# A weight load on SyncE that waits for the landing of the load two places ahead

## Chip, core and metric

The kernel runs on one core of one Trainium2 chip. The metric is the device time of one execution in microseconds; the time before is the median of three runs.

## What is computed

Attention with pooled queries, then a mixture of experts over its output. Queries are averaged in pairs, so 1152 positions give 576 tokens in each of 2 batches, 1152 tokens of width 512. Each token goes to the one expert with the largest gate logit; an expert takes at most 288 tokens.

```python
q_pool = q.reshape(B, H, S // factor, factor, D).mean(axis=3)
scores = scale * np.matmul(q_pool, k.transpose(0, 1, 3, 2))
attn = softmax(scores)
x = np.matmul(attn, v)                      # -> (N=1152, D=512)
expert_idx = np.argmax(x @ w_gate, axis=1)
gate_w = softmax(x @ w_gate)[range(N), expert_idx]
# the first `capacity` (288) tokens of each of the E=8 experts
h = np.maximum(np.einsum('ecd,edf->ecf', disp, w1), 0.0)   # w1: 8 x 512 x 1024
y = np.einsum('ecf,efd->ecd', h, w2)                       # w2: 8 x 1024 x 512
out[i] = gate_w[i] * y[expert_idx[i], pos[i]]
```

## The kernel before

The program has two parts. The first, to about 342 us, is the attention: TensorE makes scores by thirds of a row, ScalarE exponentiates, TensorE turns the result and multiplies it with v. At its end each token's expert and slot are computed, and GpSimd scatters the tokens into `xs`, a table in DRAM with 288 rows for each expert.

The second part goes through the eight experts in order. `load_x(e)` brings an expert's rows into `xe` (SyncE for expert 0, GpSimd for the others, three experts ahead). `unit(e, u)` computes a group of its tokens: `units` are 64, 64, 128 and 32 tokens. A unit of 64 is 32 matmuls with `w1` (line 824), 32 with `w2` (line 859), with turns of the intermediate result (line 838) and of the next expert's tokens (line 736) between them, and at its end `send`, in which GpSimd scatters the rows to `out` (line 762). Unit 0 is always computed. `later` puts every further unit under a condition (line 879): a flag that says whether the expert has that many tokens, which TensorE, ScalarE, VectorE and GpSimd each load into a register (`flags_of`, line 886). The path on which the unit is computed is the straight one; an engine that skips the rest of an expert's units takes the branch.

The weights are 32 loads of 1 MB (`chunks`), four for each expert: two halves of `w1`, two of `w2`. `load_w(i)` issues load i on SyncE into the buffer `wraw[i % NR]`, with `NR` = 16 buffers, so an expert's four buffers are used again four experts later. Loads 0 to 5 (`NR0` = 6) are issued during the attention, 6 and 7 behind them, and 8 to 15 when the token rows of expert 0 have been issued. After expert e come the loads of expert e + 4, each of which waits until the units that read its buffer are done:

```python
for e in range(E):
    ...
    later(e, 1, flags[e])
    if e + NX < E:
        load_x(e + NX)
    for i in range(4 * e + NR, min(4 * e + NR + 4, 4 * E)):
        load_w(i)
```

In the second part the order on SyncE, GpSimd, ScalarE and TensorE is that of the code (`manual_schedule`). SyncE takes no conditional branch: it only issues loads. Its DMAs go to one hardware queue (q1 in the profile); GpSimd's go to q0, and the engines' instructions come in pages of 16 and 8 KB on q8 and q14.

Of the kernel before, what the change touches and what calls it, by code (L numbers as in the profile page):

```python
# [10 lines left out]
I32 = mybir.dt.int32  # L11
# [11 lines left out]
MS = {mybir.EngineType.Pool, mybir.EngineType.SP, mybir.EngineType.Activation, mybir.EngineType.PE}  # L23
NR, NR0 = 16, 6
NX = 3
ENG = [mybir.EngineType.PE, mybir.EngineType.Activation, mybir.EngineType.DVE, mybir.EngineType.Pool]
FAR = 1.0e6
UT = 2
# [7 lines left out]
def attention_moe(ctx: ExitStack, tc, cap, q, k, v, wg, w1, w2, out):  # L36
    nc = tc.nc
# [536 lines left out]
    wraw = [wraw_p.tile([P, 4, 512], F32, name=f"wraw{i}") for i in range(NR0)]  # L574
# [7 lines left out]
    def load_w(i):  # L582
        e, m, c = chunks[i]
        if m == 0:
            src = w1[e].rearrange("(a p) f -> p a f", p=P)[:, :, c * 512:(c + 1) * 512]
        else:
            src = w2[e, c * 512:(c + 1) * 512, :].rearrange("(a p) d -> p a d", p=P)
        nc.sync.dma_start(out=wraw[i % NR], in_=src)

    def posts_run(f):  # L590
# [3 lines left out]
    with ExitStack():  # L594
# [34 lines left out]
        for n in range(-LEAD, 3 * NG + 20):  # L629
            p, i = divmod(n, NS)  # L630
# [29 lines left out]
            if 0 <= p < NP:  # L660
                for j in V0.get(i, ()) if p < NP - 1 else ():
                    todo.append(lambda j=j: pv_kt(p, 0, j))
                if i == XO0 and p < NP - 1:
                    todo.append(lambda: x_out(p, 0))
                if i == 26 and p % HP == HP - 1 and p < NP - 1:
                    todo.append(lambda b=p // HP: lambda: route(b, 0, 2))
                if p + 1 < NP:
                    pk, pq, p0 = (PK, PQ, 1) if p else (PK0, PQ0, PP0)
                    if i in pk:
                        todo.append(lambda: prep_k(p + 1, pk.index(i)))  # L670
                    if i in pq:
                        todo.append(lambda: prep_q(p + 1, pq.index(i)))
                    if i == p0:
                        prep_pool(p + 1)
                    if i == 22:
                        todo.append(lambda: prep_mix(p + 1))
                if p == 0 and i == 6:
                    todo.append(lambda: prep_mix(0))
                if i == 10 and p + 2 < NP:
                    load_pair(p + 2)  # L680
                if p in (1, 2) and i % 3 == 0:
                    fill()
                while fills and p == 2 and i == NS - 1:
                    fill()
                if p == NP - 2 and i % 2 == 0 and i // 2 < NR0:
                    load_w(i // 2)
# [28 lines left out]
    wraw += [ws_p.tile([P, 4, 512], F32, name=f"wraw{i}") for i in range(NR0, NR)]  # L715
    xes = [xe_p.tile([P, XB, ROW], F32, name=f"xe{i}") for i in range(NX)]
    xfs = [xe_p.tile([P, DC, XB * P], F32, name=f"xf{i}") for i in range(2)]
# [7 lines left out]
    def load_x(e):  # L725
        q = nc.gpsimd if e else nc.sync
        for s, c in blocks:
            r = e * cap + s
            q.dma_start(out=xes[e % NX][0:c, s // P, :], in_=xs[r:r + c, :])

    def trans_x(e, b):
        xe, xf = xes[e % NX], xfs[e % 2]
        c = blocks[b][1]
        ps = tr_ps.tile([P, 512], F32, tag="tr", name="xps")
        for d in range(DC):
            nc.tensor.transpose(ps[:, d * c:(d + 1) * c], xe[0:c, b, d * P:(d + 1) * P], ident[0:c, 0:c])
        nc.scalar.copy(xf[:, :, b * P:b * P + c], ps[:, 0:DC * c].rearrange("p (d c) -> p d c", c=c))

    def tags(e, u):
        o, n = units[u]  # L740
        xe, gt, it = xes[e % NX], gts[e % 4], ids[e % 4]
        src, b = slice(o % P, o % P + n), o // P
# [129 lines left out]
    def hint(e, u, flags):  # L872
        if u < NU:
            return lambda: tc.mark_branch_hint_location(f"u{e}_{u}", hint=flags[u - 1], engines=ENG)
        return lambda: None

    def later(e, u, flags):

        with tc.If(flags[u - 1] > 0, preferred_fallthrough_block=True, label=f"u{e}_{u}"):  # L879
            nxt = units[u + 1][0] if u + 1 < NU else 0  # L880
            unit(e, u, [lambda: trans_x(e, nxt // P)] if nxt and nxt % P == 0 else (), hint(e, u + 1, flags))
            if u + 1 < NU:
                later(e, u + 1, flags)

    def flags_of(e):
        flags.append(nc.values_load_multi_w_load_instructions(
            more_i[0:1, e, :], engines=ENG, min_val=0, max_val=1, skip_runtime_bounds_check_because="each is the outcome of a comparison"
        )[1])

    with tc.manual_schedule(engines=MS):  # L890
        flags = []
        flags_of(0)
        for i in range(NR0, NR0 + 2):
            load_w(i)
        for e in range(min(NX, E)):
            load_x(e)
        for i in range(NR0 + 2, min(NR, 4 * E)):
            load_w(i)
        trans_x(0, 0)
        for e in range(E):  # L900
            nxt = [lambda: trans_x(e + 1, 0), lambda: flags_of(e + 1)] if e + 1 < E else ()
            unit(e, 0, nxt, hint(e, 1, flags[e]))
# [5 lines that stand above are left out]
# [25 lines left out]
```

## Time and profile before

| | us |
|---|---|
| median of 3 runs (529.9, 533.02, 533.17) | 533.02 |
| the profiled execution | 532.41 |
| its span, first to last instruction | 530.7 |
| TensorE busy in the span | 480.1 (90%) |
| VectorE, ScalarE, GpSimd busy | 270.2, 249.5, 167.0 |
| mean granted TensorE clock | 0.975 |

The span is what the trace covers; 1.7 us of the profiled execution's own time lie around it. The shares are means over both parts; a change in the second part is to be read from the stages of that part. A matmul's idle time before it is what TensorE lost there, and the name behind it is what ended the wait, with "PEq" for TensorE's own sequencer and "issue" for time in which it waited for nothing that the profile shows. "Us to landing" of a DMA runs from its issue to the completion.

### The profile page before, as it was taken

Reading aid. Unit: us, or ns where it says so; the run is one execution under the profiler, and the core shown is the slowest. Engines: PE = TensorE matmul, PEld = TensorE weight load, DVE = VectorE, ACT = ScalarE, POOL = GpSimd, SP = SyncE. Lnnn points to the kernel's source line nnn. Section 1 sums busy time; section 2 is a strip of 40 time slices with the busy share of each in tenths; the row PEclk is TensorE's granted clock in tenths of the full one; section 3 lists DMA queues with packets and bytes.
Section 4 is the critical chain, followed back from the end, with each engine's and each line's share of the span. In section 5 each row is a group of like instructions: output and inputs, shape, how many; then the busy total and the mean of one; then the engine's idle time right before and its main releaser. Section 6 shows DMA issues by size and latency. Waiting matters only on the chain. (4 is left out here: it accounts for less than half of the span.)

```text
span 530.7 us, 9093 instructions
## 1 busy us (share of the span) xinstructions
PE 480.1 (90%) x3183; PEld 315.6 (59%) x3183; DVE 270.2 (51%) x725; ACT 249.5 (47%) x731; POOL 167.0 (31%) x290
## 2 busy tenths in 40 slices
PE   3798999999998997998999999897889998999993
PEld 2565766566666765765666766544545745574571
DVE  6587887687687898778678655600001010000100
ACT  5675866676675764766666767111112111211210
POOL 4385453243244255236035000323131132111200
PEclk9789999999999998999999999999799999999997
DMA  8899982033033132330210202389999257000000
GB/s 233 161 255 352 385 249 66 2 94 88 4 89 80 56 92 64 81 90 1 51 42 5 51 1 83 150 275 378 384 389 379 106 180 264 11 21 21 15 10 19
DMA packets 55737, 69.96 MB, mean 132 GB/s; under 512 B 21873, under 2 KB 32117, under 8 KB 55680
## 3 DMA queue, kind: packets, MB, share of 16 engines
q1 hardware_dynamic: 50320, 53.56, 32.9%
q0 software_dynamic: 4816, 15.66, 8.2%
q8 instruction: 32, 0.52, 0.4%
q14 instruction: 25, 0.20, 0.1%
q10 hardware_dynamic: 544, 0.02, 0.1%
HBM read 52.48 MB, written 11.98 MB: 121 GB/s over the span
## 5 line engine op out<-in xcount | busy, mean ns | idle before, releaser
L355 DVE TENSOR_REDUCE negm<-s 128x1 f32<-128x384 f32 x216 | 115.7, 553 | 66.3 <-PE s L350 63.3
L371 ACT ACTIVATE p<-s,negm 128x384 f32<-128x384 f32 x216 | 124.4, 583 | 39.5 <-DVE negm L359 34.0
L350 PE MATMUL s<-k,q 128*128 128x384 f32 x432 | 128.5, 389 | 10.0 <-ACT p L371 9.9
L388 PE MATMUL tp<-ident,p 128*128 128x128 f32 x648 | 109.1, 281 | 7.6 <-DVE pt L397 7.6
L413 PE MATMUL pv<-pt,vraw 128*64 128x256 f32 (+2 forms) x612 | 107.4, 407 | 0.0
L350 PEld LDWEIGHTS s<-k,q 128*128 128x128 f32 x432 | 68.1, 196 | 49.1 <-ACT p L371 32.9
L388 PEld LDWEIGHTS tp<-ident,p 128*128 128x128 f32 x648 | 81.0, 143 | 24.4 <-DVE pt L397 11.2
L399 ACT COPY pt<-tp 128x384 f32<-128x384 f32 (+1 forms) x160 | 69.9, 453 | 52.4 <-PE tp L388 51.0
L210 POOL TENSOR_TENSOR k<-kts,k 64x384 fp32r<-64x384 f32 x42 | 42.2, 1005 | 66.2 <-DVE k L209 40.3
L413 PEld LDWEIGHTS pv<-pt,vraw 128*64 128x64 f32 x612 | 41.9, 136 | 34.0 <-issue 19.4
L824 PE MATMUL hps<-wraw,xf 128*64 128x256 f32 (+1 forms) x448 | 53.2, 398 | 9.1 <-PEq L879 3.6
L253 POOL TENSOR_TENSOR q<-qts,q 64x256 fp32r<-64x256 f32 (+1 forms) x76 | 50.8, 675 | 18.0 <-DVE q L247 9.5
L762 POOL DMA_INDIRECT out_dram<-yo,id x17 | 17.1, 1007 | 120.9 <-issue 52.2
L859 PE MATMUL yps<-wraw,ht 128*64 128x256 f32 (+1 forms) x448 | 50.6, 385 | 1.2 <-DVE ht L841 1.2
L829 DVE TENSOR_SCALAR hs<-hps 128x256 f32<-128x256 f32 x12 | 5.1, 425 | 86.6 <-PE hps L824 86.6
L824 PEld LDWEIGHTS hps<-wraw,xf 128*64 128x64 f32 (+1 forms) x448 | 29.5, 137 | 28.6 <-issue 11.7
L371 ACT ACTIVATION_READ_ACCUMULATOR p<-s,negm 128x1 f32 x216 | 43.7, 202 | 0.0
L397 DVE COPY pt<-tp 128x384 f32<-128x384 f32 (+1 forms) x80 | 40.2, 511 | 6.2 <-PE tp L388 5.4
L247 DVE CAST q<-qts 64x256 fp32r<-64x256 f32 (+1 forms) x70 | 42.2, 617 | 1.1
L756 ACT ACTIVATE yo<-yps,gt 128x256 f32<-128x256 f32 (+1 forms) x15 | 7.8, 517 | 65.6 <-PE yps L859 37.1
L859 PEld LDWEIGHTS yps<-wraw,ht 128*64 128x64 f32 (+1 forms) x448 | 27.4, 133 | 17.0 <-issue 3.9
L431 POOL COPY sums<-sums 64x3 f32<-64x3 f32 x8 | 1.5, 183 | 76.4 <-ACT p L371 76.4
(117 smaller groups left out, 397.2 us busy)
## 6 DMA issues: line engine op xcount, KB each, us to landing
wraw<-in_moe_w_dram SPq DMA_DIRECT2D x32, 1024.0 KB, 14.6
vraw<-in_v_dram SPq DMA_DIRECT2D x8, 576.0 KB, 4.2
kc<-k SPq DMA_DIRECT2D x16, 288.0 KB, 3.7
xs<-zrow POOLq DMA_DIRECT2D x4, 1032.0 KB, 7.6
qraw<-in_q_dram SPq DMA_DIRECT2D x16, 256.0 KB, 3.3
kraw<-in_k_dram SPq DMA_DIRECT2D x14, 288.0 KB, 4.4
xe<-xs POOLq DMA_DIRECT2D x14, 258.0 KB, 7.1
out_dram<-zrow POOLq DMA_DIRECT2D x2, 1024.0 KB, 11.7
```

Of the source, the lines that this page charges most:

```text
L210: nc.gpsimd.tensor_tensor(out=tl[rl, c], in0=kt_s[rh, :], in1=f32(tl[rh, c]), op=ALU.subtract)
L247: nc.vector.tensor_copy(tl[r0, 0, c], qt_s[rs, a:z])
L253: nc.gpsimd.tensor_tensor(out=tl[r0, 1, c], in0=qt_s[rs, a:z], in1=f32(tl[rs, 0, c]), op=ALU.subtract)
L350: nc.tensor.matmul(ps[:, 0:CW], a, w, start=i == 0, stop=i == len(terms) - 1)
L355: nc.vector.tensor_reduce(out=negm3[g][:, j:j + 1], in_=ps[:, 0:CW], axis=AX.X, op=ALU.max, negate=True)
L371: nc.scalar.activation(pexp[g][:, j * CW:(j + 1) * CW], sthird.pop(n)[:, 0:CW], AF.Exp, bias=negm3[g][:, 3:4], scale=1.0, accum_out=sums[p ...
L388: nc.tensor.transpose(ps[:, i * P:(i + 1) * P], pexp[g][:, kt * P:(kt + 1) * P], ident)
L397: nc.vector.tensor_copy(dst, sr)
L399: nc.scalar.copy(dst, sr)
L413: nc.tensor.matmul(ps[j * D:(j + 1) * D, 0:n], vraw[:, j, kt, :], pts[p, j, src][:, kt, c0:c0 + n], start=kt == 0, stop=kt == KT - 1,)
L824: at = nc.tensor.matmul(ps[g * n:(g + 1) * n, 0:256], xf[:, d, o:o + n], raw[c // 512][:, d, c % 512:c % 512 + 256], start=d == 0, stop=d ...
L859: nc.tensor.matmul(ps[k:k + n, 0:256], ht[:, j, g * n:(g + 1) * n], raw[2 + r // 512][:, r % 512 // P, c * 256:(c + 1) * 256], start=i == ...
```

## The change

Before load i is issued, for i from 10 on, SyncE reads one word of the buffer of load i - 2 into a register. The value is not used, but the read depends on the landing of load i - 2, so SyncE stands there until that load is complete.

```diff
--- before.py
+++ after.py
@@ -23,6 +23,7 @@
 MS = {mybir.EngineType.Pool, mybir.EngineType.SP, mybir.EngineType.Activation, mybir.EngineType.PE}
 NR, NR0 = 16, 6
 NX = 3
+AHEAD = 2
 ENG = [mybir.EngineType.PE, mybir.EngineType.Activation, mybir.EngineType.DVE, mybir.EngineType.Pool]
 FAR = 1.0e6
 UT = 2
@@ -585,6 +586,12 @@
             src = w1[e].rearrange("(a p) f -> p a f", p=P)[:, :, c * 512:(c + 1) * 512]
         else:
             src = w2[e, c * 512:(c + 1) * 512, :].rearrange("(a p) d -> p a d", p=P)
+        if i >= NR0 + 2 + AHEAD:
+
+            nc.values_load_multi_w_load_instructions(
+                wraw[(i - AHEAD) % NR][0:1, 0, 0:1].bitcast(I32), engines=[mybir.EngineType.SP],
+                skip_runtime_bounds_check_because="the value is not used",
+            )
         nc.sync.dma_start(out=wraw[i % NR], in_=src)
 
     def posts_run(f):
```

No other engine's instructions change. On SyncE the first place is behind the token rows of expert 0, loads 8 (`wraw_4021`) to 15 (`wraw_4028`). The names DMAHW0 to DMAHW7 are the completion semaphores that SyncE's DMAs take in turn; load 8 signals DMAHW1, load 9 DMAHW2, load 10 DMAHW3 and so on in turn, and a row that takes a semaphore again waits for its former use. Before:

```order
L729 DMA xe_4029<-xs 32x516
L588 DMA wraw_4021<-in_moe_w_dram 128x4x512 [waits DMAHW1_49]
L588 DMA wraw_4022<-in_moe_w_dram 128x4x512 [waits DMAHW3_49]
L588 DMA wraw_4023<-in_moe_w_dram 128x4x512 [waits PE_49]
L588 DMA wraw_4024<-in_moe_w_dram 128x4x512 [waits DMAHW4_49,PE_49,Activation_49]
L879 UNCONDITIONAL_BRANCH
L588 DMA wraw_4025<-in_moe_w_dram 128x4x512 [waits DMAHW5_49]
L588 DMA wraw_4026<-in_moe_w_dram 128x4x512 [waits DMAHW6_49]
L588 DMA wraw_4027<-in_moe_w_dram 128x4x512 [waits DMAHW7_49,PE_49,Activation_49]
L588 DMA wraw_4028<-in_moe_w_dram 128x4x512 [waits DMAHW0_49,PE_49,Activation_49]
```

And with the change:

```order
L736 DMA xe_4029<-xs 32x516
L595 DMA wraw_4021<-in_moe_w_dram 128x4x512 [waits DMAHW1_49]
L595 DMA wraw_4022<-in_moe_w_dram 128x4x512 [waits DMAHW3_49]
L595 DMA wraw_4023<-in_moe_w_dram 128x4x512 [waits DMAHW1_49,PE_49]
L595 DMA wraw_4024<-in_moe_w_dram 128x4x512 [waits DMAHW2_49,DMAHW4_49,PE_49,Activation_49]
L886 UNCONDITIONAL_BRANCH
L595 DMA wraw_4025<-in_moe_w_dram 128x4x512 [waits DMAHW3_49,DMAHW5_49]
L595 DMA wraw_4026<-in_moe_w_dram 128x4x512 [waits DMAHW4_49,DMAHW6_49]
L595 DMA wraw_4027<-in_moe_w_dram 128x4x512 [waits DMAHW5_49,DMAHW7_49,PE_49,Activation_49]
L886 UNCONDITIONAL_BRANCH
L595 DMA wraw_4028<-in_moe_w_dram 128x4x512 [waits DMAHW6_49,DMAHW0_49,PE_49,Activation_49]
```

Load 9's row is the same; load 10 (`wraw_4023`) now also waits for DMAHW1, the landing of load 8, load 11 for DMAHW2, the landing of load 9, beside the former use of its own semaphore, and so on. The jump to SyncE's next stretch of code comes one load earlier.

The second place on SyncE is the last expert, loads 28 to 31, where the buffers are in their second use. Before:

```order
L588 DMA wraw_4025<-in_moe_w_dram 128x4x512 [waits DMAHW5_49,PE_49]
L588 DMA wraw_4026<-in_moe_w_dram 128x4x512 [waits DMAHW6_49,PE_49]
L588 DMA wraw_4027<-in_moe_w_dram 128x4x512 [waits DMAHW7_49,PE_49]
L879 UNCONDITIONAL_BRANCH
L588 DMA wraw_4028<-in_moe_w_dram 128x4x512 [waits DMAHW0_49,PE_49]
```

With the change:

```order
L595 DMA wraw_4025<-in_moe_w_dram 128x4x512 [waits DMAHW3_49,DMAHW5_49,SP_sequencer_49,PE_49]
L595 DMA wraw_4026<-in_moe_w_dram 128x4x512 [waits DMAHW4_49,DMAHW6_49,SP_sequencer_49,PE_49]
L886 UNCONDITIONAL_BRANCH
L595 DMA wraw_4027<-in_moe_w_dram 128x4x512 [waits DMAHW5_49,DMAHW7_49,SP_sequencer_49,PE_49]
L595 DMA wraw_4028<-in_moe_w_dram 128x4x512 [waits DMAHW6_49,DMAHW0_49,SP_sequencer_49,PE_49]
```

Here too one DMA semaphore is added to each row, and SP_sequencer beside it, SyncE's own register read of the buffer in its former use.

## Rows read from the trace of the kernel before

**Rows 1.** Engines' busy time by stage, then granted clock, DMA share and GB/s

```profile
360.00:370.00 10.00, 8.90 (x72) 5.36 (x72) 0.85 (x2) 2.10 (x5) 3.29 (x8) 1.00 1.05 378
370.00:380.00 10.00, 7.03 (x37) 3.97 (x38) 0.21 (x1) 0.76 (x2) 3.28 (x8) 0.66 1.04 381
...
410.00:420.00 10.00, 10.00 (x89) 8.85 (x88) 0.42 (x1) 1.07 (x2) 1.92 (x7) 1.00 0.52 192
```

**Rows 2.** Timeline, TensorE: start, duration, line; in brackets idle time before

```profile
366.52 2.81 PE L859 MATMUL yps<-wraw,ht 128*64 128x256 f32 x24
372.97 5.38 PE L824 MATMUL hps<-wraw,xf 128*64 128x256 f32 x24 [3.64 <-PEq L879]
...
393.87 2.38 PE L824 MATMUL hps<-wraw,xf 128*64 128x256 f32 x20 [0.74 <-DMA wraw<-in_moe_w_dram]
397.41 0.65 PE L824 MATMUL hps<-wraw,xf 128*64 128x256 f32 x4 [1.16 <-issue]
...
443.28 2.81 PE L824 MATMUL hps<-wraw,xf 128*64 128x256 f32 x24 [1.43 <-ACTq L879]
...
452.85 2.81 PE L824 MATMUL hps<-wraw,xf 128*64 128x256 f32 x24 [0.67 <-ACTq L879]
```

**Rows 3.** Branch line, TensorE's sequencer, three stretches: ns min/median/max, first and last start

```profile
L879 PEldq COMPARE_BRANCH  x1: 2563/2563/2563, 357.5 to 357.5; - x1
...
L879 PEldq COMPARE_BRANCH  x1: 5377/5377/5377, 367.2 to 367.2; - x1
...
L879 PEldq COMPARE_BRANCH  x1: 3162/3162/3162, 439.7 to 439.7; - x1
```

**Rows 4.** DMA queues in 367.2:370.0, 370.0:370.2, 394.6:394.8, 440.2:440.4: packets, MB, share

```profile
q0 software_dynamic: 168, 0.51, 48.9%
...
q8 instruction: 1, 0.02, 35.4%
...
q8 instruction: 1, 0.02, 32.9%
...
q8 instruction: 1, 0.02, 33.2%
```

**Rows 5.** Weight loads, issued 326.77, 347.93, 348.4, 353.74, 363.93, 433.51: us to landing

```profile
wraw<-in_moe_w_dram SPq DMA_DIRECT2D x1, 1024.0 KB, 5.7
...
wraw<-in_moe_w_dram SPq DMA_DIRECT2D x1, 1024.0 KB, 9.6
...
wraw<-in_moe_w_dram SPq DMA_DIRECT2D x1, 1024.0 KB, 12.6
...
wraw<-in_moe_w_dram SPq DMA_DIRECT2D x1, 1024.0 KB, 17.6
...
wraw<-in_moe_w_dram SPq DMA_DIRECT2D x1, 1024.0 KB, 20.3
...
wraw<-in_moe_w_dram SPq DMA_DIRECT2D x1, 1024.0 KB, 13.7
```

**Rows 6.** GpSimd's scatters issued at 361.12, 443.99 and 453.58: us to landing

```profile
out_dram<-yo,id POOLq DMA_INDIRECT x1, 6.4
...
out_dram<-yo,id POOLq DMA_INDIRECT x1, 3.6
...
out_dram<-yo,id POOLq DMA_INDIRECT x1, 2.5
```

**Rows 7.** Register loads on TensorE's queue: ns min/median/max, first and last start

```profile
L886 PEldq TENSOR_LOAD <-more_i x8: 768/783/1232, 343.1 to 457.6; - x8
```

**Rows 8.** Timeline, SyncE's weight loads: start, duration of the issue

```profile
347.93 0.97 SPq L588 DMA_DIRECT2D wraw<-in_moe_w_dram  x2
...
353.74 2.74 SPq L588 DMA_DIRECT2D wraw<-in_moe_w_dram  x1
...
363.93 6.78 SPq L588 DMA_DIRECT2D wraw<-in_moe_w_dram  x1
...
433.51 0.49 SPq L588 DMA_DIRECT2D wraw<-in_moe_w_dram  x1
```

## The prediction

> **What bounds the kernel now.** I read the table by stage first [rows 1]: TensorE is busy for nearly the whole of a stage, 8.90 of 10 us while weights stream (DMA share 1.05) and 10.00 when the stream ends (0.52, from 410 us on). The exception is 370 to 380 us, where TensorE is busy 7.03 of 10 us and the granted clock is 0.66. So the expert stage is bound by TensorE, and what a change of the weight queue can give is found in TensorE's pauses. The timeline of TensorE [rows 2] names them, before the first matmul of an expert: 3.64 us at 372.97, 0.74 us at 393.87, 1.43 us at 443.28, 0.67 us at 452.85, and one of 1.16 us in the middle of a run of matmuls at 397.41. Two things go with the long one. It is put down to TensorE's own sequencer, not to data. And the 24 matmuls behind it take 5.38 us where the same 24 take 2.81 us at 443.28: the clock had fallen while the engine stood still. That is 2.6 us more.
>
> What the sequencer did is in the rows of the branch at the end of each expert's units [rows 3]. Where the branch leaves the straight path it takes 2.56, 5.38 and 3.16 us. It is reached some 2 us before TensorE has finished (367.2 against 366.52 + 2.81 = 369.33), so the first 2 us are hidden and the rest is the pause. The DMA rows tell why one is long [rows 4]: from the branch at 367.2 to 370.0 no instruction packet moves, only weights (q1) and token rows (q0); the packet begins at 370.0, 2.8 us late, and the branch ends 2.6 us after it. At 439.7 the packet begins at 440.2, 0.5 us after the branch, and the branch ends 2.7 us after it. So the pause is a code page that arrives late, and the part that differs is the time before its packet starts.
>
> How full the weight queue is at these moments: the load issued at 353.74 [rows 8] lands 17.6 us later (371.3) and the one at 363.93 lands 20.3 us later (384.2) [rows 5], so at 367.2 five loads of 1 MB (12 to 16) are queued. At 439.7 two are left of four, the last issued at 433.51 and landing 13.7 us later (447.2), at 2.7 us each. Other small transfers show the same dependence [rows 6]: GpSimd's scatter of results lands in 6.4 us at 361 (five loads queued), 3.6 at 443.99 (little more than one), 2.5 at 453 (none).
>
> **The change part by part.** The wait: each load from number 10 on is issued only when the load two places back has landed (the order of SyncE shows the added semaphores, and nothing moves on any other engine). A register load from SBUF carries the wait; on SyncE none is in the trace, on TensorE's queue the same operation takes 0.77 to 1.23 us, 0.78 in the median [rows 7], so I take 0.8 and keep 0 to 1.3 as bounds. Behind the waiting instruction on SyncE stand only further weight loads; the one other user of that queue, the token rows of expert 0, is issued before. No engine waits for SyncE except for the weights.
>
> Does any weight come late? A load alone lands 5.7 us after issue [rows 5]. At full stream, 381 GB/s [rows 1], 1 MB (1.05 million bytes) costs 2.75 us, say 2.7. With two in flight, a load lands at the later of (the one before) + 2.7 and (the one two before) + 0.8 + 5.7. Loads 8 and 9 are queued as now and land at 347.93 + 9.6 = 357.5 and about 348.4 + 12.6 = 361.0 [rows 5, 8]. From there 10 lands at 364.0, 11 at 367.5, and so on with 6.5 us for each two: 13 at 374.0, 15 at 380.5, 19 at 393.5, 23 at 406.5, 27 at 419.5, some 5 us behind the end of the stream now [rows 1]. They are wanted for expert 2 at 372.97 (second half, loads 10 and 11, 4 us later), expert 3 at 393.87, expert 5 at 443.28, expert 6 at 452.85 [rows 2]; those of expert 4 (16 to 19) are there before expert 3 begins; the smallest slack is about 6 us, where load 11 at 367.5 meets a need at 374 with the pause gone. Loads 28 to 31 are issued when expert 3 is done, and load 31 lands near 447, before expert 6 begins, for expert 7. So the wait itself costs nothing, and what hides it is the stock of sixteen buffers. If a pair took 16 us in place of 6.5, the cover would be gone.
>
> What it gives: at 367.2 the queue would hold load 11 (ending) and load 12 (issued about 364.8), between one and two loads in place of five. The row nearest to one load is 3.6 against 2.5 us idle, 1.1 us of delay; twice that, an estimate, for two loads. I take the middle, 1.65, against the 2.8 of now: the pause at 372.97 falls by 1.2, from 3.64 to 2.4 us. As bounds: all of the 2.8, with which the pause would come near the 0.7 of the ordinary ones (a gain of 2.9), and nothing. The clock: it fell in a pause of 3.64 and was not low after one of 1.43 (24 matmuls in 2.81 at 443.28). 2.4 lies between; I take half of the 2.6, 1.3, and keep 0 and 2.6. The pause of 1.16 us at 397.41 has its code page in the same stream (the packet at 394.6 [rows 4]); a page 1.2 us sooner removes it: 1.2, with 0 as the other end. The pauses of 0.67 to 1.43 stay: those at 443.28 and 452.85 are at a short queue already.
>
> Sum: 1.2 + 1.3 + 1.2 = 3.7 us. The profiled execution took 532.41 us (span 530.7 and 1.7 around it), so 528.7. The median of the runs, 533.02, is 0.6 above it, and its lowest, 529.9, is 3.1 below that: some executions may escape part of this pause already. About 1% (5.3 us) is what a measurement of this kernel can tell from no change; the forecast is inside that.
>
> [...]
>
> **The rivals.** [...]
>
> *Everything is recovered.* The packet starts at once as at 440.2, the pause falls to 0.7, the clock stays: 2.9 + 2.6 + 1.2 = 6.7, so 525.7.
>
> *The queue runs dry and weights come late (slower).* From load 10 on each pair needs a full landing, a register load and an issue in turn. Place: expert 6, the end of the longest chain. Load 27 is used at about 457.5; it is nine pairs behind load 9, so a pair may take (457.5 - 361.0) / 9 = 10.7 us, which is 5 us of turnaround beside the 5.7. Above that TensorE waits nine times the excess: at 6 us of turnaround 9 us, 541. The 0.77 to 1.23 us of the register loads are far from 5; against that, no such load on SyncE is in the trace.
>
> *The change does not hold the loads back.* The order shows the semaphore of load 8 in front of load 10, so this has next to no chance; it would give 533.
>
> **How the numbers follow.** Forecast (part of the pauses goes, 526.5 to 531.5) 0.50; depth does not matter (531.5 to 534) 0.30; everything recovered (524.5 to 526.5) 0.12; late weights (over 538) 0.08. The predicted time is the first, 528.7. The range, 525.5 to 534, leaves out the late weights and half of the full recovery. Faster by over 1% is below 527.7: the 0.12 and about a third of the forecast's own range, 0.18, so 0.30. Slower by over 1% is 0.08. Within 1%, 0.62.
>
> **What would show it.** On SyncE, DMA issues from load 10 on that take 0.4 us each in place of 2.7 to 6.8 [rows 8] and landings near 6 us in place of 14 to 20. In the DMA row a share near 0.8 from 360 to 415 us, and a stream that ends near 420. The branch of expert 1 at about 367 taking 4 us or less, and no low clock from 370 to 377. I would be wrong if that branch still takes over 5 us with short landings (depth does not matter), or if matmuls wait for weights in experts 3 to 6 (late weights).

## The result, and the profile after

The median of 21 runs with the change is 532.21 us, against 533.17 for 21 runs of the kernel before in the same comparison. A gain is not shown clearly. The ratio of the runs is 0.9902, with a 95% interval of 0.9875 to 0.9929, but it leaves out runs more than 1.5% above the fastest of their kernel, which takes away 11 of the 21 here because the changed kernel scatters so much, and so favours it. Over all runs the means are 531.5 and 533.0 us: 1.5 us or 0.3% apart, with a standard error of 1.0 us. The scatter is the plainer result: 524.0 to 540.3 us with the change, 528.6 to 535.9 before (standard deviations of 4.3 and 1.8 us).

The execution whose trace is shown took 540.26 us (span 538.6), the longest of the 21. First SyncE: all weight loads (the columns are ns min/median/max, first and last start), and their landings.

```profile
L595 SPq DMA_DIRECT2D wraw<-in_moe_w_dram x32: 367/368/1604, 7.4 to 440.8; - x32
...
DMA to landing us min/median/max: 5.9/7.9/15.8
```

SyncE's waits on landings, in total us, times and longest:

```profile
SPq L591 <- DMA wraw<-in_moe_w_dram: 72.2, 21, 8.7
```

The held-back loads do what was said. The issue takes 0.37 us, where it took up to 6.8 in a full queue [rows 8]; the median landing is 7.9 us, and loads landed after 17 to 20 us before [rows 5]. The wait stands 72.2 us in 21 places on SyncE, and TensorE waits for no weight. From landing to next issue it takes about 0.1 us (load 10, issued at 357.61, lands 6.3 us later, at 363.9; load 12 is issued at 363.96). The read of a word itself is not in the trace: in its line stand semaphore instructions of 17 ns, and SyncE shows no register load.

```profile
L591 SPq EVENT_SEMAPHORE  x22: 17/17/17, 357.5 to 440.7; - x22
```

Then the stages, with columns as in [rows 1]: TensorE first, then granted clock, DMA share and GB/s at the end of a row.

```profile
360.00:370.00 10.00, 9.31 (x80) 5.34 (x76) 0.85 (x2) 1.81 (x4) 3.29 (x8) 1.00 1.02 360
370.00:380.00 10.00, 6.59 (x46) 4.11 (x42) 0.00 (x0) 0.86 (x2) 3.28 (x8) 0.83 0.98 336
...
410.00:420.00 10.00, 10.00 (x90) 8.27 (x87) 0.43 (x1) 1.37 (x3) 1.91 (x7) 1.00 0.93 323
...
440.00:450.00 10.00, 4.74 (x35) 2.95 (x36) 0.42 (x1) 0.47 (x1) 3.23 (x8) 0.85 0.88 278
450.00:460.00 10.00, 9.76 (x66) 5.18 (x62) 0.85 (x2) 1.49 (x4) 0.05 (x1) 0.81 0.08 28
```

The gap at 370 to 380 is still there: TensorE is busy for 6.59 of 10 us, 7.03 before. A second has come at 440 to 450, with 4.74 of 10 us and a granted clock below 1 on both sides. From 410 to 420 the weights still stream (0.93, 0.52 before). TensorE's timeline, the branch in its sequencer and the instruction queue (0.2 us from 372.2 and from 445.0) at these places, to be set beside [rows 2 to 4]:

```profile
375.19 4.50 PE L831 MATMUL hps<-wraw,xf 128*64 128x256 f32 x24 [3.41 <-PEq L886]
...
398.38 0.65 PE L831 MATMUL hps<-wraw,xf 128*64 128x256 f32 x4 [0.87 <-issue]
...
448.08 5.39 PE L831 MATMUL hps<-wraw,xf 128*64 128x256 f32 x24 [5.26 <-PEq L886]
...
460.69 2.81 PE L831 MATMUL hps<-wraw,xf 128*64 128x256 f32 x24 [0.93 <-PEq L886]
```

```profile
L886 PEldq COMPARE_BRANCH  x1: 5117/5117/5117, 369.6 to 369.6; - x1
...
L886 PEldq COMPARE_BRANCH  x1: 7002/7002/7002, 440.7 to 440.7; - x1
```

```profile
q8 instruction: 1, 0.02, 34.9%
...
q8 instruction: 1, 0.02, 33.8%
```

The branch of expert 1 takes 5.12 us (5.38 before), and the pause before expert 2 is 3.41 us (3.64). Its code page starts at 372.3, 2.7 us after the branch, where it was 2.8: next to nothing was gained there. The branch of expert 4 takes 7.00 us in place of 3.16; its page starts at 445.1, 4.5 us after the branch, and expert 5 begins after a pause of 5.26 us with the clock down: 24 matmuls take 5.39 us at a granted clock of 0.50 (448.08 to 453.47), where in the kernel before they took 2.81 at 1.00 (443.28 to 446.09).

There are traces of three more executions of the same kernel (below). In all four the pause at expert 2 is there (3.41, 3.58, 4.22 and 3.93 us), and in three of the four the one at expert 5 has grown (5.26, 5.65 and 4.57 us; 0.67 in the other, 1.43 before).

### The profile page after: what moved, and what is told of

Its sections match the earlier page's. It is cut to its first block, busy times and chain, and to the rows that moved or that the text cites. A ratio compares the mean times of both kernels' runs of the same rounds, so it can differ in the third digit from the quotient of the medians.

```text
span 538.6 us, 9112 instructions
## 1 busy us (share of the span) xinstructions
PE 485.1 (90%) x3183; PEld 318.8 (59%) x3183; DVE 270.1 (50%) x725; ACT 249.3 (46%) x731; POOL 167.1 (31%) x290
## 5 line engine op out<-in xcount | busy, mean ns | idle before, releaser
L831 PE MATMUL hps<-wraw,xf 128*64 128x256 f32 (+1 forms) x448 | 54.9, 407 | 12.6 <-PEq L886 9.6
L831 PEld LDWEIGHTS hps<-wraw,xf 128*64 128x64 f32 (+1 forms) x448 | 30.9, 141 | 32.4 <-issue 16.9
```

What stands on the lines that cost most here:

```text
L831: at = nc.tensor.matmul(ps[g * n:(g + 1) * n, 0:256], xf[:, d, o:o + n], raw[c // 512][:, d, c % 512:c % 512 + 256], start=d == 0, stop=d ...
```

## The experiments

Two measures recur. A *page turn* is the time from the start of one 16 KB instruction packet on q8 to the next, read from the DMA view in windows of 0.1 us; the turns that count are those from the page that ends expert 0's branch on, where TensorE needs one page after the other. The pages' rows name no engine; they are taken for TensorE's because its branches that wait over 1 us end 2.3 to 2.7 us after one of them starts, in every trace. The *pause* is TensorE's idle time before the first matmul of experts 2 and 5. Page turns and pauses are those of one trace for each kernel, the times those of all its runs. Runs of the kernel before were taken anew for each group of comparisons.

| kernel | runs | mean us (range) | before | ratio (95%) | page turns, experts 0 to 2 | pause at 2, at 5 |
|---|---|---|---|---|---|---|
| before | 21 | 533.0 (528.6 to 535.9) | | | 6.0, 6.5, 6.0 | 3.64, 1.43 |
| the change | 21 | 531.5 (524.0 to 540.3) | 533.0 | 0.9902 (0.9875 to 0.9929) | 6.0, 7.1, 6.4 | 3.41, 5.26 |
| no_stream | 6 | 524.3 (521.2 to 526.3) | 532.7 | 0.9856 (0.9810 to 0.9902) | 4.3, 3.8 | 0.67, 0.67 |
| ahead1 | 4 | 539.4 (538.4 to 540.9) | 532.7 | 1.0135 (1.0083 to 1.0187) | 5.9, 6.0, 4.8 | 0.67, 0.67 |
| ahead4 | 12 | 532.0 (526.3 to 536.9) | 532.7 | 0.9977 (0.9941 to 1.0014) | 6.0, 6.9, 6.0 | 3.77, 3.48 |
| tokens_sync | 12 | 528.9 (524.3 to 531.6) | 532.7 | 0.9933 (0.9897 to 0.9970) | 6.0, 6.4, 6.0 | 3.48, 0.67 |
| after_tok | 12 | 532.3 (529.5 to 535.6) | 533.2 | 0.9981 (0.9949 to 1.0013) | 4.7, 6.3, 3.5 | 1.69, 0.67 |
| fill1 | 9 | 530.5 (528.3 to 532.5) | 533.2 | 0.9944 (0.9914 to 0.9975) | 6.0, 6.3, 6.1 | 0.41, 0.67 |
| tok_fill | 12 | 530.6 (528.3 to 533.3) | 533.5 | 0.9955 (0.9923 to 0.9987) | 6.0, 6.4, 6.0 | 0.41, 0.67 |
| after_act | 12 | 528.0 (524.0 to 531.9) | 533.5 | 0.9914 (0.9874 to 0.9953) | 3.5, 6.5, 5.0 | 0.67, 0.67 |
| before_act | 12 | 534.1 (529.9 to 536.6) | 533.5 | 1.0008 (0.9975 to 1.0041) | 6.0, 6.6, 6.0 | 3.48, 0.67 |

### What makes the page late: weights, their depth, or token rows

**no_stream** (the kernel before without most of the weights):

```diff
-        raw = [wraw[(4 * e + c) % NR] for c in range(4)]
+        raw = [wraw[(4 * e + c) % 8] for c in range(4)]
...
-        for i in range(NR0 + 2, min(NR, 4 * E)):
+        for i in range(0):
...
-            for i in range(4 * e + NR, min(4 * e + NR + 4, 4 * E)):
+            for i in range(0):
```

> The kernel before without loads 8 to 31: experts 2 to 7 multiply with the weights of experts 0 and 1, so their part of the output is not the reference's. Token rows and scatters stay. If code pages are late because weight loads are queued (by depth or merely because any weights move): every branch of TensorE takes 2.7 us or less, the pauses of 3.64 and 1.16 us and the low clock are gone, 525 to 526.5 us, and the runs lie within 3 us of each other. If they are late because of GpSimd's token rows: the branch of expert 1 still takes 4 to 7 us, 530 to 533.

Its mean is 524.3 us. TensorE's timeline at experts 2 and 5, and the branch of expert 1:

```profile
368.85 2.81 PE L824 MATMUL hps<-wraw,xf 128*64 128x256 f32 x24 [0.67 <-ACTq L879]
...
434.25 2.81 PE L824 MATMUL hps<-wraw,xf 128*64 128x256 f32 x24 [0.67 <-ACTq L879]
```

```profile
L879 PEldq COMPARE_BRANCH  x1: 344/344/344, 366.0 to 366.0; - x1
```

Pauses of 0.67 and a branch of 0.34 us: the page is there before the branch is reached. The token rows, which stay, do not make it late by themselves; with the weights gone it is not late. The 8.4 us between the means are an estimate of the most that any order of the loads could give here. Two things were not as expected: the runs lie within 5.1 us, not 3, so not all of the scatter comes with the weights, and the mean is somewhat below 525.

**ahead1** and **ahead4** are the change with `AHEAD = 1` and `AHEAD = 4`.

> The change with one load in flight (wait for the load one place ahead, from load 9 on). Landings every 6.5 us by the sum of the prediction (5.7 + 0.8), so load 11 lands near 377, load 15 near 403, load 23 near 455 and load 27 near 481: late by 2, 4, 8 and 12 us, 545 us or more, with TensorE waiting for weights in experts 2, 3, 5 and 6. If a turn is shorter (4.5 us), nothing is late but a little at expert 2, and with the least depth of all the time is 525 to 528 by depth, 530 to 533 if depth does not matter.

> The change with four loads in flight. By depth: four loads are 10 us of queue, so pages are late much as before, 531 to 533, with the narrow spread of the kernel before. If what matters is only that SyncE issues in step with landings, not how deep the queue is: like the change, a wide spread from 524 to 540 with a mean near 531.

ahead1 was slower by 1.3%, 539.4 us, less than the 545 expected: loads 9 to 12 were issued 5.2 to 5.8 us apart, less than 6.5. TensorE's waits for weights, in total us, times and longest, and its timeline at expert 2:

```profile
PE yps L866 <- DMA wraw<-in_moe_w_dram: 4.5, 2, 3.0
PE hps L831 <- DMA wraw<-in_moe_w_dram: 1.4, 1, 1.4
```

```profile
371.22 2.81 PE L831 MATMUL hps<-wraw,xf 128*64 128x256 f32 x24 [0.67 <-ACTq L886]
...
452.19 5.38 PE L831 MATMUL hps<-wraw,xf 128*64 128x256 f32 x22 [1.43 <-DMA wraw<-in_moe_w_dram]
```

So one load in flight is too few, and the price comes where the prediction's slower rival put it, at expert 6 (waits of 1.4 and 3.0 us, a page's 2.0 us, and a low clock behind them), besides 1.45 us in expert 3. The pause at expert 2 is gone. The page turns do not say that this is for lack of depth: the first is 5.9 us with one load in flight and 6.0 with two, four and the full queue (in one of four executions of the change it is 4.2), the second 6.0 with one, 7.1 to 8.2 with two, 6.9 with four and 6.3 to 6.6 with the full queue. Without weights the two are 4.3 and 3.8. What is different with one in flight is that the first of these pages starts 4.6 us after expert 0's first matmul in place of 6.8 (5.9 to 6.8 with two in flight), while the DMA engines have gaps (a share of 0.73 from 350 to 360 us, 0.99 with two in flight and 1.02 before). From two loads on, fewer loads did not make the page of expert 2 come sooner; the one trace with one load in flight does not settle it there.

ahead4 gave no gain that can be told from none, and its range, 10.6 us, lies between the 8.7 of the kernel before in this comparison and the 16 of the change. Both pauses are there, and the one at expert 5 has grown as with two in flight:

```profile
372.35 4.39 PE L831 MATMUL hps<-wraw,xf 128*64 128x256 f32 x24 [3.77 <-PEq L886]
...
443.62 4.50 PE L831 MATMUL hps<-wraw,xf 128*64 128x256 f32 x24 [3.48 <-PEq L886]
```

### Pages in series: work put into TensorE's pause

A unit takes 8.7 us (452.85 to 461.59 in the kernel before), and the first two page turns there are 6.0 and 6.5 us. If a unit uses two pages, an estimate from these numbers is that the pages are the bound wherever two experts with one unit follow each other, and that what TensorE does meanwhile costs nothing, up to the length of the pause. **fill1** puts five matmuls without use there, in the kernel before:

```diff
+        if (e, u) == (1, 0):
+            fill_ps = h_ps.tile([P, 512], F32, tag="h", name="fill")
+            for _ in range(5):
+                nc.tensor.matmul(
+                    fill_ps, ident, wgi.rearrange("p c w -> p (c w)")[:, 0:512], start=True, stop=True
+                )
         send(e, u, ps)
```

> The kernel before with 5 matmuls of 512 columns (592 ns each, 3.0 us) behind expert 1's unit on TensorE, whose result is not used. If the code pages come one behind the other, some 6 us apart while weights stream, whatever TensorE does, the page of expert 2 arrives when it did, the 3 us lie in the pause of 3.64, the clock stays up (2.6 us) and the time falls to 530 to 531. If the page is fetched only when the branch is reached, it moves by 3 us, the pause stays and the time rises to 535 to 536.

```profile
368.77 4.56 PE L873 MATMUL fill<-wgi,ident 128*128 128x512 f32 x10
...
373.74 2.81 PE L824 MATMUL hps<-wraw,xf 128*64 128x256 f32 x24 [0.41 <-PEq L885]
```

```profile
L885 PEldq COMPARE_BRANCH  x1: 4497/4497/4497, 367.4 to 367.4; - x1
```

The page started at 369.3, 9.4 us after the start of expert 1; before, at 370.1, it was 9.6 us. So it did not move, though TensorE had 4.56 us more to do (in the trace the five calls are ten matmuls, more than the 3.0 us I had put down). The pause is 0.41 us and the 24 matmuls behind it take 2.81 us, for the clock stayed up (granted 1.00 from 370 to 380 us, 0.66 before). From the start of expert 1 to expert 2's second unit it is 22.5 us, against 23.9 before (384.28 - 360.42): added work made this stretch 1.3 us shorter. Since 4.56 us are more than the pause, expert 2 began 1.3 us later, and the clock gave back 2.6. Over the runs the mean fell by 2.7 us, more than this stretch accounts for.

This run does not refute the other theory, a page that is fetched only when its branch is reached. TensorE's sequencer was ahead of the matmuls: it reached the branch at 367.4, before the added matmuls began (368.77) and 7.5 us after the start of expert 1 (359.94), 6.8 before, so the branch moved by 0.7 us only. no_stream does refute it. The program announces its branches: `hint` puts two BRANCH_PREFETCH_HINT instructions on TensorE's queue in each first unit. In expert 1 of the kernel before, and of no_stream with the page of the same branch (the instruction queue in 0.2 us from 361.3):

```profile
L929 PEldq BRANCH_PREFETCH_HINT  x2: 30/32/34, 360.5 to 363.0; - x2
...
L929 PEldq BRANCH_PREFETCH_HINT  x2: 30/30/30, 359.4 to 361.8; - x2
q8 instruction: 1, 0.02, 33.9%
```

Without weights this page starts 2.0 us after the first hint and 4.7 us before the branch at 366.0. In the kernel before it starts 9.6 us after the first hint (370.1), behind the page of 363.6. That the hint asks for it fits the order; a kernel without hints was not run. A turn of 6.0 us has two parts: a waiting branch ends about 2.5 us after its page starts, and the next page starts 3.5 us after that (360.1 to 363.6 and 372.5 to 376.1 in the kernel before). The second part is 3.4 to 3.6 us at these two places in all kernels with a full queue and with four loads in flight, 0.9 to 3.9 with two in flight, 2.5 and 3.2 with one, and 0.7 without weights. So holding loads back to two did shorten this part at times; with the change alone the page behind it, the one of expert 2, then waited longer (turns of 7.1 to 8.2).

### The token rows, and the second pause

**tokens_sync** issues them on SyncE, in the kernel before; **after_tok** does the same with the change; **before_act** and **after_act** use ScalarE's queue:

```diff
-        q = nc.gpsimd if e else nc.sync
+        q = nc.sync
```

```diff
-        q = nc.gpsimd if e else nc.sync
+        q = nc.scalar if e else nc.sync
```

> The kernel before, deep weight queue, with the token rows of experts 1 to 7 issued on SyncE in place of GpSimd, so that GpSimd's queue holds only the small scatters. If the depth of the weight queue makes the pages late: no change, 532 to 534, the branch of expert 1 at 5 us or more, since five loads are queued as before. If the token rows on the second queue make them late: the branches fall to 2.7 us or less, 526 to 528.

> The change, and the token rows of experts 1 to 7 issued on SyncE too. If the wide spread of the change comes from a code page that meets GpSimd's token rows (9.3 us from one page to the next at expert 4), the spread narrows to that of tokens_sync (524 to 532) and the mean falls to 527 to 529. If the held-back loads alone make it, the spread stays at 524 to 540 and the mean near 531.5.

> The change, with the token rows of experts 1 to 7 issued on ScalarE's hardware queue at the place where GpSimd issued them. If GpSimd's queue together with held-back loads makes the page of expert 5 late (9.3 to 9.7 us after the one before), it comes 6 to 6.5 us after it here, the pause of 5.3 to 5.7 is gone, and with token rows in time (not 7 us late as in after_tok) the mean is 526 to 528. If any token rows beside held-back loads do it, the pause stays and the mean is near 531.5. ScalarE waits on SyncE's semaphores for its issues, which may cost some us.

> The kernel before, loads not held back, with the token rows of experts 1 to 7 on ScalarE's queue as in after_act. If the gain of after_act (mean 528.0 against 533.5) is that of the token rows' place, the mean is 528 to 529 here too, with page turns of 6.0 to 6.5 us. If held-back loads are needed for it, page turns of 6.0 to 6.5 leave the pause of 3.5 us at expert 2 and the mean is 531 to 533.

tokens_sync gained 0.7% (528.9 us) with the pause at expert 2 as it was, so neither theory had it right: its gain is not in the page of expert 2. That page was as late with no token rows on GpSimd's queue. The trace, of an execution of 526.63 us, has the pause at expert 5 at 0.67, but 4.0 of the 5.8 us by which it is shorter than the one before lie ahead of expert 0's first matmul, which starts at 346.77 (350.80 before):

```profile
346.77 2.81 PE L824 MATMUL hps<-wraw,xf 128*64 128x256 f32 x24 [0.72 <-ACT xf L737]
...
368.75 5.39 PE L824 MATMUL hps<-wraw,xf 128*64 128x256 f32 x24 [3.48 <-PEq L879]
...
438.91 2.81 PE L824 MATMUL hps<-wraw,xf 128*64 128x256 f32 x24 [0.67 <-ACTq L879]
```

after_tok shows both sides. The pauses are 1.69 and 0.67 us, and the spread is narrow (529.5 to 535.6), as the first theory had it. But the mean was 532.3, not 527 to 529, because the token rows now stand on SyncE behind loads that wait for landings, and come late:

```profile
369.70 2.81 PE L831 MATMUL hps<-wraw,xf 128*64 128x256 f32 x24 [1.69 <-PEq L886]
...
381.02 1.09 PE L743 MATMUL xps<-ident,xe 128*128 128x128 f32 x4 [7.13 <-DMA xe<-xs]
...
444.81 2.81 PE L831 MATMUL hps<-wraw,xf 128*64 128x256 f32 x24 [0.67 <-ACTq L886]
```

The 7.13 us wait for `xe` is more than the pauses give back.

after_act avoids that wait and has the lowest mean of all versions that load all weights, 528.0 us against 533.5 before and 531.5 with the change, and no long pause at experts 2 and 5 in its trace, but one of 3.59 us at expert 6. The trace is of the shortest of its 12 runs, 524.04 us, and here too 4.4 of the 8.4 us by which it is shorter lie ahead of expert 0's first matmul (346.38):

```profile
366.17 2.81 PE L831 MATMUL hps<-wraw,xf 128*64 128x256 f32 x24 [0.67 <-ACTq L886]
...
432.78 2.81 PE L831 MATMUL hps<-wraw,xf 128*64 128x256 f32 x24 [0.67 <-ACTq L886]
...
445.87 2.81 PE L831 MATMUL hps<-wraw,xf 128*64 128x256 f32 x24 [3.59 <-PEq L886]
```

before_act has no gain at all (534.1 against 533.5), with page turns of 6.0, 6.6 and 6.0 us and pauses of 3.48 us at expert 2 and 3.58 at expert 6:

```profile
373.40 5.39 PE L824 MATMUL hps<-wraw,xf 128*64 128x256 f32 x24 [3.48 <-PEq L879]
...
454.37 4.45 PE L824 MATMUL hps<-wraw,xf 128*64 128x256 f32 x24 [3.58 <-PEq L879]
```

So held-back loads and token rows on ScalarE's queue are worth 1% together, where ScalarE's queue alone is worth nothing; SyncE's alone was worth 0.7%. That the 1% comes from the two pauses is not shown, since half of the trace's gain lies elsewhere. The expectation that GpSimd's queue alone makes the second late page falls: in after_act such a page came late too (9.4 us behind the one before), one expert further on.

**tok_fill** is tokens_sync and fill1 together.

> The kernel before with token rows on SyncE and the 5 idle matmuls behind expert 1's unit: both kernels' gains together. tokens_sync still had the pause of 3.48 us and the low clock at expert 2; with pages in series the matmuls cover the pause as they did in fill1 and the clock stays up: 2.6 us less than the mean of tokens_sync (528.9), so 526 to 527, below both kernels. If the two gains are the same one, 528 to 530.

It came to 530.6 us, no better than fill1; the gains did not add. The pause at expert 2 was filled, but the one in the middle of expert 3 (put down to "issue") was 2.11 us in its trace (1.42 in tokens_sync, 1.84 in fill1). From expert 0's first matmul to the end its trace takes 177.9 us, as long as that of tokens_sync (178.0); why the filled pause did not show there is open beyond these 0.7 us:

```profile
373.21 2.81 PE L824 MATMUL hps<-wraw,xf 128*64 128x256 f32 x24 [0.41 <-PEq L885]
...
395.57 1.73 PE L824 MATMUL hps<-wraw,xf 128*64 128x256 f32 x13 [2.11 <-issue]
```

### The changed kernel again

> The change again, for one more execution's pages. If pages in series bound the one-unit experts, each page begins 3.8 to 7 us behind the one before, and the pauses of experts 2 and 5 are what this leaves behind a unit's 8.7 us; no page waits longer because more loads are queued. If depth decides, pages begin within 1 to 2 us of their branch.

> The change again. A time of 524 to 527 would show which of the two pauses is absent in the short executions: by pages in series both page turns are then 5 us or less (no_stream 3.8 to 4.3). A time of 530 to 534 would have one of the two pauses, over 536 both with low clock.

> The change again, with the same expectation as after_look2: 524 to 527 without pauses at experts 2 and 5, 530 to 534 with one of them, over 536 with both.

The three took 538.25, 529.93 and 535.92 us. The rows at experts 2 and 5, of each in turn:

```profile
373.37 5.39 PE L831 MATMUL hps<-wraw,xf 128*64 128x256 f32 x24 [3.58 <-PEq L886]
...
446.71 4.89 PE L831 MATMUL hps<-wraw,xf 128*64 128x256 f32 x24 [5.65 <-PEq L886]
```

```profile
373.91 4.16 PE L831 MATMUL hps<-wraw,xf 128*64 128x256 f32 x24 [4.22 <-PEq L886]
...
440.79 2.81 PE L831 MATMUL hps<-wraw,xf 128*64 128x256 f32 x24 [0.67 <-ACTq L886]
```

```profile
371.69 5.31 PE L831 MATMUL hps<-wraw,xf 128*64 128x256 f32 x24 [3.93 <-PEq L886]
...
445.15 4.43 PE L831 MATMUL hps<-wraw,xf 128*64 128x256 f32 x24 [4.57 <-PEq L886]
```

Their page turns from expert 0 on are 4.2, 8.2, 3.6; then 6.0, 7.6, 4.4; then 5.9, 7.2, 3.8 us. In the five kernels with a full weight queue (before, tokens_sync, fill1, tok_fill, before_act) the same three turns are 6.0, 6.3 to 6.6, and 6.0 to 6.1: nearly the same every time. Held-back loads let some turns fall to 3.5 to 4.4 us, near the 3.8 to 4.3 without weights, and make others 7 to 8, and at expert 5 up to 9.7 (433.9 to 443.6 in the first of the three). So the first expectation, 3.8 to 7 us from page to page, missed both 8.2 and 9.7; pages within 1 to 2 us of their branch, the other theory's sign, did not come either (2.8 us at expert 1). The shortest of the three, 529.93, has no long pause at expert 5. None of them fell among the six of the 21 runs at 524 to 527.3, so which pause those lack is not shown.

## Why the prediction was right, and where its steps failed

The time, 532.21, lies in the range, but not in the forecast's own part of it (526.5 to 531.5): it lies where the rival "depth does not matter" had put it. The cause of the pauses was read rightly from the trace before: a code page that comes late while weights stream. no_stream shows this. The step that failed is the next one, that the delay of the page shrinks with the number of loads queued.

- *The pause at expert 2, 3.64 to 2.4 us.* It was 3.41 to 4.22 in four executions. A shorter queue did not bring the page sooner: of the two turns before it the first is 6.0 us with four and with all loads queued and mostly so with two, and the second is longer with two and four (7.1 to 8.2 and 6.9) than with all (6.3 to 6.6). The two rows I leaned on, scatters that landed in 6.4 and 3.6 us, measure another thing, GpSimd's small writes. And a delay measured from the branch was the wrong quantity, since pages follow each other, a page can start before its branch is reached, and the branch only shows what is left over. The rival "depth does not matter" was right about this pause, with two and with four loads in flight; that the token rows make this page late was not shown (tokens_sync has them on another queue and the pause stays, 3.48 us).
- *The clock, 1.3 of 2.6 us.* The pause stayed, and so did the low clock: 4.50, 5.39, 4.16 and 5.31 us for the 24 matmuls, 5.38 before.
- *The wait in the middle of expert 3, 1.16 to 0.* It was 0.87, 0, 0 and 1.31: about half of the term.
- *The pause at expert 5, "stays" at 1.43.* This was the worst. It became 4.57 to 5.65 in three of four executions, with the clock down behind it. I had read it as a short queue already; but the full-queue traces have 0.67 to 1.43 there and the change up to 5.65 with no more loads queued, so a short queue was not what kept it small. Page turns near it range from 3.6 to 9.7 us with held-back loads.
- *The wait itself at no cost.* Right, with its terms off: TensorE waited for no weights; the turnaround was 0.1 us where I had taken 0.8, with semaphore instructions of 17 ns and no register load in SyncE's trace, but landings took 7.9 us in the median, not near 6, and loads 10 to 13 landed at 7.6 us for each two in place of 6.5. Load 11 had landed before 367.65, when load 13 could go, and expert 2 began at 375.19. The rival of late weights came true with one load in flight only.

So the sum of 3.7 us did not come: the runs show 1.0 us in the median and 1.5 in the mean, not clear of nothing, and that the time lies in the range is in part luck, as gains in some executions meet losses in others. In the execution of 529.93 the stretch from the first matmul of expert 0 to the end of the span is 177.0 us (528.2 - 351.2), against 179.9 before (530.7 - 350.8): the pause at expert 5 is 0.8 shorter, the wait in expert 3 is gone (1.2), the clock came back earlier (1.2), and the pause at expert 2 is 0.6 longer. In the other three it is 184.9 to 185.3, five more than before. The attention part adds scatter of its own: the first matmul of expert 0 starts between 349.3 and 353.3 us in these four, and between 346.4 and 353.3 over all traces.

Where weights moved, the taken branches of experts 1 and 4 stood 5.12 and 7.00 us in the execution above; without weights the same two took 0.34 us each (at 366.0 and 431.4 in no_stream), the first with its page started 4.7 us before it. With no load left a branch stood at its page too: in the kernel before the one at 450.0 took 2.29 us, with its page from 449.9 on. The pause at expert 2 was about the same with two, four and all loads queued (3.41 to 4.22, 3.77 and 3.64 us); the turns of 7 to 9.7 us with held-back loads are not explained by that.

Open stays why held-back loads spread the page turns, and so why the page at expert 5 comes so late. Loads 30 and 31 are then issued one at a time, at 438.27 and 440.81, just around the branch at 440.7, where before all four of this expert's loads were issued by 434.0. That alone is not the cause: in the execution of 529.93 they were issued as close to the branch (435.08 and 437.71, the branch at 437.96), and the page came 3.6 us after the one before; in ahead4 all four were issued by 431.9, and the pause is 3.48 us. Nor is a late page there peculiar to held-back loads: before_act holds none back and has turns of 8.7 and 7.6 us and the pause of 3.58 at expert 6.

## What to carry to other kernels

A pause that a trace puts down to an engine's own sequencer behind a branch should be read as a series: list the instruction packets and take the time from one to the next, before asking what delays a single one. A page can start long before its branch (4.7 us in no_stream), so a wait counted from the branch says little. Work put into such a pause can pay: in fill1, 4.56 us of matmuls in a pause of 3.64 kept the granted clock at 1.00 (0.66 before), and the stretch became 1.3 us shorter. Holding back the other traffic to two loads moved the packets about here (in four traces of the change first turns of 4.2 to 6.0 us and second ones of 7.1 to 8.2, against 6.0 and 6.5 before) without a clear gain. And a change that makes a kernel scatter more has to be judged over all its runs and several profiles, since one profile shows one draw, and a chosen set of the shorter runs shows a gain that all runs do not.

## What the runs showed of the hardware

- Where one-unit experts follow each other (experts 0 and 1), instruction pages of 16 KB for TensorE follow each other after 3.8 to 4.3 us without weight loads (no_stream) and 6.0 to 6.6 us beside a full queue of them (five kernels). In the kernel before two pages then take 12.5 us (6.0 and 6.5), longer than an expert of one unit, 9.6 us from start to start without the long pause (350.80 to 360.42).
- With no weight loads (no_stream) the page of expert 1's branch started 4.7 us before the branch was reached, 2.0 us after a BRANCH_PREFETCH_HINT; with a full queue (the kernel before), 9.6 us after the hint.
- More work made a stretch shorter: 4.56 us of matmuls in a pause of 3.64 saved 1.3 us, as the granted clock did not fall (1.00 from 370 to 380 us in fill1, 0.66 before).
- Holding loads back to two in flight raised the scatter of a kernel's time from 7 to 16 us over 21 runs each, with the same bytes moved.
- The wait on a landing cost about 0.1 us on SyncE: a semaphore instruction of 17 ns stands there, and no register load, which takes 0.78 us on TensorE [rows 7].
